# GLA recurrence and tanh-shrink MLP: fewer DMA pieces for w_in, another load order for unit 0, fewer warming products, new instruction orders

## The chip, the cores and the metric

The kernel runs on one core of one Trainium2 chip. The metric is the device time of one execution in microseconds; the median of three runs is given. Five engines matter: TensorE (PE in the profile; its weight loads are shown as PEld), VectorE (DVE), ScalarE (ACT), GpSimd (POOL) and SyncE (SP), which issues nearly all DMA transfers.

## The reference

```python
B, H, S, D = 4, 8, 768, 48            # d_model = H*D = 384, d_ff = 2048
for t in range(S):                    # gated linear attention
    state = alpha[:, :, t, :, None] * state + einsum('bhd,bhe->bhde', k[:, :, t], v[:, :, t])
    y[:, :, t] = einsum('bhd,bhde->bhe', q[:, :, t], state)
x = y.transpose(0, 2, 1, 3).reshape(B * S, H * D)
h = x @ w_in                          # (3072 x 384) @ (384 x 2048)
g = h - tanh(h)
out = g @ w_out                       # (3072 x 2048) @ (2048 x 384)
```

The inputs q, k, v and alpha are float32. w_in and w_out arrive as float64, seen as 64-bit integers, and are rebuilt as float32 on the chip.

## The kernel before

**Units and steps.** The 3072 tokens are cut into twelve units of 256 tokens (two chunks of 128), numbered 0 to 11. Each unit first passes the recurrence: turn or transpose alpha, k and q so that features lie on partitions (`turn aT`, `turn kT`, `turn qT` by TensorE for units 0 and 1, line 717; `flip` on DVE for the others, line 689); two scans along time on DVE (`U`, line 760, and `W`, line 779); k times U and q times W (line 729 or 784); then matmuls for scores, the update of the state and y. Then it passes eight MLP steps, numbered `u:s` (0:0 is unit 0, step 0). A step's first product is `first` (line 1242: twelve PE records, 2.59 us; plain form), ACT and DVE work on h (`square`, `cube`, `quad`, `shrunk`), and the second product follows (`second`, line 1322 for units 0 and 1, line 1344 afterwards with fewer multiplications). In all there are 96 steps.

**Weights.** w_in and w_out come in eight pieces each, `in0` to `in7` and `out0` to `out7`; a piece is 768 KB. `fetch` issues its DMA (line 42), ACT reads the raw words in two passes (`read`, lines 85 and 86), and DVE finishes the conversion in two more (lines 88 and 89). `first 0:s` needs `in<s>`, `second 0:s` needs `out<s>`. There are four raw buffers, so a fetch waits until DVE's first pass over the piece four places earlier is done. A piece of w_in is cut by tile and row range: eight DMAs of 96 KB. A piece of w_out is one DMA.

**Order.** The order of the work is written out by hand, or rather by a search whose result is stored: `Planner.STEPS` is a list of differences that gives the order in which all tasks are emitted, and so each engine's own order. The planner knows a cost (`us`) and a latency (`lat`) for each task. From them it works out starts only to decide where to put extra work on PE: `filler` is `spin`, a 128x128 product of the identity with itself (line 1428) whose result nobody reads. It fills PE's planned gaps until `y 0.0`. The before kernel has 36 spins: 8, then 2, 7, 10, 5, 2 and 2 at seven places.

**Loads of unit 0 and 1.** For unit 0 the loads of alpha, q, v and k, in this order, are issued in halves from SP and from ACT's queue. Then SP issues `in0`, and for unit 1 alpha, v, k, q, then `in1`, `in2`, `in3`. For units from 2 on (and alpha of unit 1) each of `ar`, `kr` and `qr` is loaded by four DMAs of 96 KB (line 607).

**DMA slots.** DMAs issued from SP and ACT share eight completion semaphores in turn. An issue waits until the transfer eight places before it has landed.

Of the kernel before, what the change touches and what calls it, by code (L numbers as in the profile page):

```python
# [17 lines left out]
HP = 64  # L18
# [19 lines left out]
def load_weight(nc, pool, rows, **kw):  # L38

    raw = pool.tile([P, WN], I64 if rows[0][2].dtype != FP32 else FP32, name="raw", **kw)  # L40
    for at, js, src in rows:
        nc.sync.dma_start(out=raw[at].rearrange("p (j n) -> p j n", n=src.shape[-1])[:, js], in_=src)
    return raw


def weight_parts(w_in, w_out, pad_rows, what, s, by_tile=True):

    if what == "out":
        return [(slice(0, P), slice(0, 2), w_out.rearrange("(j p) n -> p j n", p=P)[:, 2 * s:2 * s + 2, :])]
    parts = []  # L50
    for i in range(len(pad_rows[0])):
        at, f0 = pad_rows[0][i]
        step = pad_rows[1][i][1] - f0
        src = w_in[f0:f0 + len(pad_rows) * step].rearrange("(j p) n -> p j n", p=step)
        src = src[0:at.stop - at.start, :, 2 * s * P:2 * (s + 1) * P]

        few = at.stop - at.start < 32 or not by_tile
        parts += [(0, at, slice(0, len(pad_rows)), src)] if few else [(j - 9, at, slice(j, j + 1), src[:, j:j + 1]) for j in range(len(pad_rows))]
    return [x[1:] for x in sorted(parts, key=lambda x: (x[0], x[1].start))]
# [261 lines left out]
class Planner:  # L321
# [6 lines left out]
        "90 2 1 1 -3 9 -3 -1 -96 106 8 -11 -8 12 2 1 -6 4 -10 7 12 15 -14 -17 10 -12 20 -17 33 -23 8 -119 122 5 5 -20 8 8 5 -132 122 -9 27 -139 119 3 -9 27 -13 "  # L328
        "383 -382 13 -7 -11 -120 141 -2 3 -2 -10 -9 387 -510 134 16 -15 -130 506 -375 9 -8 9 -145 512 -366 365 -509 513 -2 -506 -4 144 369 -506 -5 512 5 -372 "
        "-2 3 367 -361 -149 -2 149 -142 506 -367 371 -514 511 8 -512 509 -1 -513 147 368 -367 -3 358 -500 -2 7 510 -514 520 -382 380 -511 508 1 -377 -137 504 "  # L330
        "11 4 -518 2 140 -135 512 4 -3 -517 140 -133 -5 139 377 -12 15 -518 2 5 512 5 -4 -517 519 -512 511 -516 505 -497 512 -519 2 132 386 4 -519 -2 7 511 "
        "-515 504 -502 125 389 3 -516 508 10 2 -3 -388 390 -392 387 -512 128 -4 397 -520 156 -24 394 -5 2 -398 397 -392 3 391 -365 374 -399 4 -10 16 383 -9 "
        "-387 403 -395 -10 400 -371 367 -365 359 9 3 -374 -21 400 3 -9 5 -400 2 395 8 -3 -376 381 -378 -24 404 -3 -351 356 -380 -4 -21 402 9 -380 -7 382 2 -382 "
        "25 -23 379 -406 411 -390 392 -17 -344 -49 405 -359 366 -387 375 -402 411 -408 410 -407 2 47 -30 383 -404 3 46 -48 4 -151 172 1 -3 388 -384 -173 174 "
        "-173 557 2 -1 -3 -554 189 -15 -25 1 -149 150 410 -2 -384 -2 387 -380 382 -369 371 -557 559 -3 -385 17 27 347 -4 -389 47 -42 -2 3 -5 14 376 3 2 -1 -350 "
        "-213 188 380 -349 -218 559 5 -373 2 382 -10 3 -348 -32 381 -3 -377 381 6 -4 -373 -4 383 -386 24 366 -5 -387 6 375 8 -385 379 -376 386 -3 -579 -8 581 "
        "-359 369 1 -410 42 -43 -172 585 3 -4 -410 46 375 -6 2 -5 -360 364 -371 360 -335 352 2 2 -404 50 341 5 -591 220 372 -370 374 6 -601 196 401 -377 26 346 "
        "7 3 -377 -2 377 4 -1 -353 -35 393 -3 -362 -242 221 384 11 -8 -412 -195 -12 621 2 -3 -3 -405 416 -6 -621 629 -6 10 -376 371 2 1 -619 629 -7 -621 625 -3 "
        "-11 18 -6 7 1 -7 11 -23 -416 436 4 -10 12 -1 3 -7 -14 -425 3 -196 198 -4 5 26 401 12 -637 639 -419 421 -420 427 -6 2 -1 -642 644 -423 424 3 -647 649 "
        "-1 -18 21 -453 23 -24 40 -14 18 413 -455 451 -426 15 399 17 2 -428 40 -25 417 -660 267 388 -406 -2 422 -8 -4 -656 662 -419 418 3 -14 25 -6 -12 -385 "  # L340
        "-31 430 -28 33 -6 -402 2 -26 436 -29 -650 662 -416 436 -6 1 -676 663 -416 423 -427 428 -15 -384 410 2 -461 460 -6 2 -15 -438 -5 1 2 -223 247 417 23 "
        "-439 -247 683 1 10 -7 2 -1 3 -443 447 2 -1 5 -700 264 4 -44 24 -247 248 420 -403 435 4 -408 -47 458 -437 25 393 -12 -400 -5 430 1 -430 436 6 -713 695 "
        "-472 485 -484 485 -27 -410 417 25 -438 -23 443 22 -450 422 -390 -299 701 -406 2 -24 423 13 6 -12 -453 464 -4 6 -444 449 -473 -247 250 -2 4 465 10 -6 "
        "-468 -252 278 21 422 1 -448 453 -25 29 -3 -453 454 -20 14 1 -723 716 13 2 -730 274 442 16 -440 -40 -1 43 -41 24 446 -424 434 -732 738 -5 1 -412 -48 30 "
        "-27 458 -453 454 10 -745 738 -770 772 -1 3 34 -24 -6 -5 7 -452 29 404 18 -424 430 -10 14 -3 -18 -442 461 -754 748 11 -438 434 -6 8 9 -466 460 -432 433 "
        "-462 -2 465 -464 478 -9 -24 34 -8 2 -3 -467 477 -452 468 -44 13 32 -827 811 -476 461 16 16 -26 -12 23 16 -25 10 16 -15 16 1 -16 17 -16 28 -11 -15 -22 "
        "49 -28 17 -15 17 -1 3 8 -26 42 -58 43 -10 26 -24 9 16 -59 44 16 -15 16 -15 16 1 -16 17 -16 28 -11 -15 -34 61 -28 -32 49 -15 27 -10 -564 563 12 -9 -18 "
        "28 -62 -513 -3 517 -516 578 -574 528 34 13 -574 563 12 -549 -4 554 -48 -505 563 19 -28 -48 58 -57 48 28 -27 9 -43 44 -9 27 -17 -44 62 -27 10 18 -62 63 "
        "-18 19 -18 19 -18 -46 65 -18 -571 573 -1 18 -16 1 16 8 -582 -16 -24 563 -562 622 -59 -538 589 -16 -597 622 -59 -538 598 -59 -522 -14 586 -584 594 -9 "
        "-36 -509 555 -45 -540 586 1 13 -59 -512 -43 556 46 -30 -553 554 30 12 -10 28 -17 -42 33 -32 29 13 -27 -567 611 -16 -27 -542 557 13 16 -43 -574 575 43 "  # L350
        "-16 -573 590 -16 1 -14 30 -593 -20 -24 638 -634 618 17 -637 621 28 -632 589 32 -15 -599 626 -28 17 -621 649 -26 10 -44 61 -16 -44 -583 644 -16 -44 31 "
        "30 -16 -30 19 28 -16 -45 46 16 -624 625 1 -17 -634 602 61 -28 -16 45 -61 33 1 28 -61 17 45 -61 47 15 -61 32 30 -15 28 -683 671 -12 13 -16 28 -43 -17 "
        "33 28 -12 -48 61 -688 660 -32 48 -669 655 16 -1 12 -60 -605 -16 1 681 -706 660 -634 -25 30 676 -661 -44 706 -47 48 -47 1 -621 668 10 18 -24 -35 -605 "
        "637 -31 41 18 -44 -14 31 10 -678 696 -58 41 -651 669 -17 18 -17 18 -30 13 32 -14 -671 654 -31 49 -30 -635 617 31 -30 48 -17 30 -712 652 48 -47 60 -29 "
        "46 -16 -12 -33 14 32 -45 61 -30 -695 710 16 -47 -14 1 61 -729 713 -688 705 -16 -32 33 16 -732 700 -672 705 -735 719 17 -33 1 44 -62 51 -17 29 -62 -686 "
        "737 28 -44 28 -62 79 -78 62 -9 -21 47 -16 -47 34 14 -47 63 -46 17 -736 750 -748 749 -31 46 -63 34 30 -63 48 16 -63 64 -16 2 -778 777 16 -49 35 -781 5 "
        "801 -803 793 -49 -741 801 17 -823 797 -1 11 -8 -772 4 732 -16 77 -76 33 27 -780 797 -61 34 28 -17 -44 35 10 17 -61 62 -17 1 17 -16 17 -16 -785 802 -15 "
        "-1 17 4 -3 9 -795 720 -735 -25 -1 24 752 61 -26 -809 852 -26 10 -811 750 35 43 -16 -61 -746 824 -809 793 -61 78 -16 17 -63 64 -17 -13 -786 817 -17 18 "
        "-17 -48 78 -29 -815 817 15 -31 32 -17 29 -10 -68 -766 -3 770 66 12 -63 54 -19 29 16 -860 816 29 -64 80 -79 -781 11 834 16 -79 64 16 -15 16 -31 16 16 "
        "-850 851 1 -68 51 -829 779 -781 782 78 -28 17 -66 51 -18 -18 63 -11 28 -901 20 865 -8 -55 34 18 -847 859 -11 -17 -35 79 -15 -866 803 -796 812 48 15 "  # L360
        "-62 63 -45 30 -863 864 -14 -852 881 -63 64 -63 48 16 -63 48 -863 865 -16 30 -902 887 -33 -853 888 -887 853 48 -47 34 -33 47 10 -890 882 26 -27 10 -42 "
        "35 -883 891 -9 -33 -848 891 -42 34 24 -57 -849 907 -918 902 -886 859 44 -16 17 -44 97 -52 -17 1 17 -16 17 -16 28 -11 -15 -32 1 58 -28 17 28 -43 27 -10 "
        "-33 32 12 16 -59 16 18 10 -43 32 27 -15 -43 59 -26 11 16 -15 16 1 -16 17 -16 30 -13 -15 -34 63 -30 -32 49 -15 -33 50 12 16 -29 3 -51 33 -17 62 -28 12 "
        "-45 35 11 16 -61 46 -45 61 1 -16 17 -16 17 -16 17 -16 -969 986 -15 -1 17 -15 17 8 -9 3 -56 -932 -4 937 -935 997 -1000 939 36 26 -61 62 15 -25 11 -47 "
# [64 lines left out]
def fast(tc, q, k, v, alpha, moe_w_in, moe_w_out, out, w_in, w_out, ident, ok, pad_rows):  # L429
    nc = tc.nc  # L430
# [1111 lines left out]
```

## Time and profile before

| | |
|---|---|
| Three runs | 564.53, 565.50, 565.52 us; median 565.5 us |
| The profiled execution | 566.18 us; its span from first to last instruction is 564.5 us |
| Busy in the span | PE 553.1 us (98%), PEld 502.9, DVE 463.9, ACT 358.7, POOL 4.9 |
| Mean granted TensorE clock | 0.993 |
| DMA | 50.90 MB in 60717 packets, mean 90 GB/s |
| Products of `spin` | 36 |

Busy time is the time in which an engine has an instruction in it; for PE the ends of matmuls are modelled. "Idle before, releaser" in a row tells how long the engine had nothing to do and which instruction's end let it go on. A matmul of float32 stands as two records, so 8 spins are a row of x16. A busy PE is not the same as useful PE: spins count as busy.

### The profile page before, as it was taken

How to read it: one execution, taken by the hardware profiler on the slowest of the kernel's cores; microseconds unless marked ns; L12 is line 12 of the kernel's file. 1: busy time of each engine (PE TensorE's matmuls, PEld its weight loads, DVE VectorE, ACT ScalarE, POOL GpSimd, SP SyncE). 2: the span in 40 equal slices, each digit the busy share in tenths (PEclk: the TensorE clock that was granted, in tenths of full speed). 3: DMA queues.
4: the chain of work that ended last, by engine and by line, in shares of the span. 5: the costliest groups of instructions: out<-in, count | busy, mean ns of one | idle time of the engine just before them, and what ended most of it. 6: DMA issues, size and time to landing. Idle time of an engine off the chain costs nothing.

```text
span 564.5 us, 14803 instructions
## 1 busy us (share of the span) xinstructions
PE 553.1 (98%) x6029; PEld 502.9 (89%) x6029; DVE 463.9 (82%) x855; ACT 358.7 (64%) x723; POOL 4.9 (1%) x23
## 2 busy tenths in 40 slices
PE   8989999999999999999999999999999999999995
PEld 8877777678999999999999999899999999999994
DVE  6879789999997598796996779999979975765764
ACT  2579988737876668777575446857745555455550
POOL 3000000000000000000000000000000000000000
PEclk9989999999999999999999999999999999999998
DMA  7777873229464275563430013031110000000001
GB/s 197 209 211 220 273 189 113 59 64 198 92 143 126 88 134 137 141 160 97 130 107 1 31 35 88 29 83 38 32 36 2 29 9 1 30 9 1 28 1 35
DMA packets 60717, 50.90 MB, mean 90 GB/s; under 512 B 35776, under 2 KB 50400, under 8 KB 60640
## 3 DMA queue, kind: packets, MB, share of 16 engines
q1 hardware_dynamic: 57728, 48.88, 33.2%
q10 hardware_dynamic: 2912, 0.98, 0.7%
q8 instruction: 49, 0.80, 0.6%
q14 instruction: 28, 0.23, 0.1%
HBM read 44.04 MB, written 4.72 MB: 86 GB/s over the span
## 4 chain that ended last, share of the span: by engine, by line
PE 94%; DVE 3%; issue 1%; ACT 0%; POOL 0%; DVEq 0%; ACTq 0%; POOLq 0%
PE o L1344 32%; PE h L1242 22%; PE h L1253 13%; PE o L1322 7%; PE h L1274 7%; PE h L975 4%; PE spin L1428 2%; PE sc L948 2%; PE sc L1121 1%; PE sc L955 1%; PE sc L975 1%; PE turned L717 1%; DVE same L1407 1%; DVE W L779 0%; DVE U L760 0%
## 5 line engine op out<-in xcount | busy, mean ns | idle before, releaser
L1242 PE MATMUL h<-xT,w_in 128*128 128x256 f32 (+1 forms) x588 | 132.9, 380 | 1.7 <-DVE w_in L89 1.6
L1242 PEld LDWEIGHTS h<-xT,w_in 128*128 128x128 f32 x588 | 109.8, 192 | 18.0 <-DVE w_in L89 2.7
L1344 PE MATMUL o<-b,e 128*128 128x192 f32 x480 | 94.2, 326 | 0.0
L1344 PEld LDWEIGHTS o<-b,e 128*128 128x128 f32 x480 | 78.8, 191 | 0.2
L1344 PE MATMUL o<-w_out,e 128*128 128x192 f32 x320 | 78.8, 328 | 0.0
L1298 DVE SCALAR_TENSOR_TENSOR g<-z,w 128x512 f32<-128x512 f32 x96 | 65.2, 681 | 4.3 <-ACT z L1289 1.6
L1344 PE MATMUL o<-b,g 128*128 128x192 f32 x320 | 68.4, 326 | 0.0
L1279 DVE TENSOR_TENSOR w<-h,u 128x512 f32<-128x512 f32 x48 | 32.9, 686 | 36.7 <-PE h L1274 36.7
L1289 ACT ACTIVATE z<-u 128x512 f32<-128x512 f32 x96 | 60.1, 629 | 1.8
L1285 ACT ACTIVATE u<-w 128x512 f32<-128x512 f32 x48 | 30.2, 630 | 41.3 <-DVE w L1279 41.3
L1253 PE MATMUL h<-xT,w_in 128*128 128x128 f32 x288 | 55.5, 279 | 0.9 <-DVE w L1279 0.6
L1344 PEld LDWEIGHTS o<-w_out,e 128*128 128x128 f32 x320 | 55.1, 190 | 1.3
L1253 PE MATMUL h<-xT,w_out 128*128 128x128 f32 x288 | 54.1, 275 | 0.0
L1344 PEld LDWEIGHTS o<-b,g 128*128 128x128 f32 x320 | 54.0, 190 | 0.1
L1285 ACT ACTIVATE u<-h 128x512 f32<-128x512 f32 x48 | 28.3, 592 | 40.0 <-PE h L1242 39.7
L1253 PEld LDWEIGHTS h<-xT,w_in 128*128 128x128 f32 x288 | 48.4, 190 | 4.2 <-DVE w L1279 1.5
L1266 ACT COPY u<-h 128x128 f32<-128x128 f32 x96 | 24.5, 265 | 43.0 <-PE h L1253 42.6
L1304 ACT ACTIVATE big<-u 128x1024 f32<-128x1024 f32 x48 | 50.6, 1054 | 0.5
L1274 PE MATMUL h<-xT,w_in 128*128 128x256 f32 x192 | 49.0, 380 | 0.0
L1311 DVE TENSOR_TENSOR e<-g 128x384 f32<-128x384 f32 x80 | 44.0, 550 | 3.4 <-PE o L1344 1.1
L1294 DVE TENSOR_TENSOR w<-h,u 128x512 f32<-128x512 f32 x48 | 32.7, 680 | 15.0 <-ACT u L1285 15.0
L1253 PEld LDWEIGHTS h<-xT,w_out 128*128 128x128 f32 x288 | 44.3, 192 | 0.1
(167 smaller groups left out, 979.9 us busy)
## 6 DMA issues: line engine op xcount, KB each, us to landing
raw<-in_moe_w_out_dram SPq DMA_DIRECT2D x16, 768.0 KB, 5.3
raw<-in_moe_w_in_dram SPq DMA_DIRECT2D x80, 96.0 KB, 3.7
raw<-in_moe_w_in_dram SPq DMA_DIRECT2D x16, 288.0 KB, 5.2
vt<-in_v_dram SPq DMA_DIRECT2D x23, 192.0 KB, 3.6
ar<-in_alpha_dram SPq DMA_DIRECT2D x44, 96.0 KB, 2.3
qr<-in_q_dram SPq DMA_DIRECT2D x40, 96.0 KB, 2.3
kr<-in_k_dram SPq DMA_DIRECT2D x40, 96.0 KB, 2.2
out_dram<-cross SPq DMA_DIRECT2D x19, 96.0 KB, 1.7
```

The lines of the kernel that those rows point to most:

```text
L1242: T.matmul(h[:, a, to], lhsT=w_in[:, j, f * P:(f + 1) * P], rhs=xT[u][:, j, to], start=(j == 0), stop=(j == KT - 1))
L1253: T.matmul(m["h", s][:, to], lhsT=left[n][:, s], rhs=right[u][n], start=start, stop=True, skip_group_check=True)
L1274: T.matmul(m["h", s][:, 2 * a:2 * a + 2].rearrange("p i t -> p (i t)"), lhsT=wi[:, KT - 1, s, a], rhs=xT[u][:, KT - 1, :], start=False, st ...
L1279: V.tensor_add(m["w", s], m["h", s].rearrange("p i t -> p (i t)"), m["u", s])
L1285: A.activation(m["u", s], m["h", s], AF.Square, scale=W_SCALE ** -1.5)
L1289: A.activation(m["z", s], m["u", s], AF.Square, bias=QB, scale=QA * W_SCALE)
L1294: V.tensor_mul(m["w", s], m["h", s], m["u", s])
L1298: V.scalar_tensor_tensor(out=g.rearrange("p a c t -> p (a c t)"), in0=m["z", s], scalar=QK, in1=m["w", s], op0=ALU.add, op1=ALU.mult)
L1304: A.activation(big, m["us", s // 2].rearrange("p s t -> p (s t)"), AF.Relu, bias=-U_FAST, scale=W_SCALE, accum_out=over[:, n:n + 1])
L1311: V.tensor_sub(e[:, 0:3, :], x[:, 3:4].to_broadcast([P, 3, P]), x[:, 0:3])
L1322: T.matmul(m["o"][c], lhsT=g[:, a, c, :], rhs=w_out[:, f, :], start=(f == 0), stop=(f == FT - 1))
L1344: T.matmul(o[n][:, i], lhsT=g_, rhs=w_, start=(s_ == 0 and (n, i) in ((0, 0), (1, 0), (2, 1), (3, 0))), stop=(s_ == FS - 1), skip_group_ch ...
```

## The change

- `load_weight` and `weight_parts`: a piece of w_in is six DMAs rather than eight. For the two ranges of 48 rows, tile 0 is one DMA of 96 KB and tiles 1 and 2 together one of 192 KB; the two ranges of 16 rows stay as they were. Of piece `in0` alone, the two DMAs of the upper range of 48 rows (partition 64) are issued from ACT's queue.
- `load`: `ar`, `kr` and `qr` take two DMAs of 192 KB per load rather than four of 96 KB.
- `filler`: another rule for the number of spins. The program now has 23: 7 ahead of `turn aT 0`, 15 ahead of `back 0.0`, 1 ahead of `update 0.0`.
- New planner costs for loads and fetches, `turn aT 0` at 1.5, and one more planned dependency for `scores 1.0`.
- `STEPS` is new. Among much else: unit 0 is loaded as alpha, k, q, v; unit 1 as q, alpha, k, v; the three turns of unit 0 stand one after another; ACT reads `in0` before it copies `kn` of chunk 0.0 (line 1039), DVE finishes `in0` before it masks the scores of 0.0, `in1` before `kU` of unit 1 and `in2` before the `W` scan of unit 1; PE runs `first 0:1` before `back 1`, and `first 0:3` and `second 0:0` before `scores 1.0`.

Besides these, each engine has the same instructions as before: PE's only other count is the 13 spins, DVE's is the same, ACT has two more DMA issues, SP 96 fewer.

```diff
-def load_weight(nc, pool, rows, **kw):
+def load_weight(nc, pool, rows, both=False, **kw):
     for at, js, src in rows:
-        nc.sync.dma_start(out=raw[at].rearrange("p (j n) -> p j n", n=src.shape[-1])[:, js], in_=src)
+        (nc.scalar if both and at.start % HP == 0 and at.start else nc.sync).dma_start(
+            out=raw[at].rearrange("p (j n) -> p j n", n=src.shape[-1])[:, js], in_=src)
...
-        parts += [(0, at, slice(0, len(pad_rows)), src)] if few else [(j - 9, at, slice(j, j + 1), src[:, j:j + 1]) for j in range(len(pad_rows))]
+        parts += [(0, at, slice(0, len(pad_rows)), src)] if few else [(j - 9, at, slice(j, k), src[:, j:k]) for j, k in ((0, 1), (1, len(pad_rows)))]
...
     STEPS = (
-        "90 2 1 1 -3 9 -3 -1 -96 106 8 -11 -8 12 2 1 -6 4 -10 7 12 15 -14 -17 10 -12 20 -17 33 -23 8 -119 122 5 5 -20 8 8 5 -132 122 -9 27 -139 119 3 -9 27 -13 "
+        "90 1 1 2 -1 2 -95 100 -3 9 -10 7 11 -7 27 -30 6 -1 -4 27 -34 -97 98 18 16 -32 11 -4 10 17 -33 17 -117 135 -17 -117 139 -14 -15 8 -10 12 6 14 -28 9 "
...
-                filled += [(free, -1, do, None)] * int(gap / (1.5 * us) if free == self.begin.get(engine) else (gap + 0.3) / us if gap > 0.2 else 0)
+                filled += [(free, -1, do, None)] * int(gap / (1.75 * us) if free == self.begin.get(engine) else gap / us - 1 if gap > 2 * us else 0)
...
+    BOTH_QUEUES = 1
...
-            raw_of[what, s] = load_weight(nc, raw_pool, weight_parts(moe_w_in, moe_w_out, pad_rows, what, s), bufs=4)
+            raw_of[what, s] = load_weight(nc, raw_pool, weight_parts(moe_w_in, moe_w_out, pad_rows, what, s), both=what == "in" and s < BOTH_QUEUES, bufs=4)
...
-                for g in (0, NP // 2):
-                    nc.sync.dma_start(out=t[HP * r:HP * r + 32, g:g + 2].rearrange("p g t d -> p g (t d)"),
-                                      in_=src[head(g, r):head(g, r) + 2].rearrange("g (i n) -> i g n", i=32))
+                nc.sync.dma_start(out=t[HP * r:HP * r + 32].rearrange("p g t d -> p g (t d)"),
+                                  in_=src[head(0, r):head(0, r) + NP].rearrange("g (i n) -> i g n", i=32))
```

## The prediction

> **What bounds the kernel now.** I read the page's busy row and slices first, then the sums by stretch, then the order in time of PE, DVE and SP over the first 60 us, and the waits.
>
> ```profile
> PE 553.1 (98%) x6029; PEld 502.9 (89%) x6029; DVE 463.9 (82%) x855; ACT 358.7 (64%) x723; POOL 4.9 (1%) x23
> ...
> PEclk9989999999999999999999999999999999999998
> ```
>
> PE is busy for 98% of the span, and the clock row shows one dip, in the third slice.
>
> ```profile
> 31.05:37.66 6.61, 4.65 (x18) 3.54 (x17) 4.64 (x8) 4.91 (x9) 0.00 (x0) 0.74 0.86 242
> 37.66:45.00 7.34, 7.26 (x210) 6.01 (x209) 5.65 (x11) 6.27 (x10) 0.00 (x0) 1.00 0.57 172
> 45.00:557.70 512.70, 511.82 (x5245) 467.12 (x5245) 428.92 (x791) 334.01 (x683) 0.00 (x0) 1.00 0.31 81
> ```
>
> These are sums by stretch: length, then busy time of PE, PEld, DVE, ACT, POOL, then granted clock, DMA share, GB/s. From 45 us to the last product at 557.7 PE lacks only 0.88 us. The change leaves PE's instructions there as they are, so what is won must come mainly from the first 45 us, by handing PE the same work earlier. From 31.05 to 37.66 PE idles 2 us and its clock is 0.74.
>
> ```profile
> 1.57 3.79 PE L1428 MATMUL spin<-ident 128*128 128x128 f32 x16 [1.57 <-POOL ident masks.py:199]
> 5.28 1.89 PE L717 MATMUL turned<-ident,rough 64*64 64x64 f32 x64
> ...
> 8.84 1.83 PE L1428 MATMUL spin<-ident 128*128 128x128 f32 x14
> 10.59 1.55 PE L717 MATMUL turned<-ident,rough 64*64 64x64 f32 x64
> 12.07 2.50 PE L1428 MATMUL spin<-ident 128*128 128x128 f32 x20
> 14.41 0.55 PE L1034 MATMUL y<-ident,kT 112*128 112x112 f32 x4
> ...
> 29.60 1.60 PE L1242 MATMUL h<-xT,w_in 128*128 128x128 f32 x12
> 31.05 0.55 PE L1121 MATMUL y<-ident,kT 112*128 112x112 f32 x4
> 31.97 0.60 PE L1121 MATMUL y<-ident,kT 112*128 112x112 f32 x4 [0.37 <-DVE kT L729]
> 34.15 4.54 PE L1242 MATMUL h<-xT,w_in 128*128 128x256 f32 x12 [1.58 <-DVE w_in L89]
> ```
>
> PE in order of time: start, length, operation. Four losses stand here. Ten spins hold `back 0.0` until 14.41, though its input is ready at 12.76:
>
> ```profile
> 12.09 0.67 DVE L729 TENSOR_TENSOR kT<-turned,U 128x512 f32<-128x512 f32 x1
> ...
> 33.14 0.96 DVE L89 CUSTOM_DVE_ANT_0 w_in<-bits,more 128x1536 uint16<-128x1536 uint16 x1 [0.17 <-DVE bits L88]
> ```
>
> The second turn (k, loaded last, landed at 9.37 by the DMA records) lasts 1.55 against 1.16 for that of q. `first 0:1` waits 1.58 us for `in1`, which DVE finishes only at 34.1 though its bytes landed at 25.03. And that product takes 4.54 us where the form takes 2.59: after the idle stretch the clock stood at 0.50 for 3.41 us (34.24 to 37.66).
>
> **Part by part: start.** A cold spin costs (3.71 - 0.26)/8 = 0.43 us; a warm one 0.245 (ten from 12.07 to 14.41, seven from 8.84 to 10.59, five in 1.23). Spins before: 3.71 + 0.64 + 1.75 + 2.34 + 1.23 + 0.64 + 0.82 = 11.13 us from start to next start. After: 7 cold 3.28, 15 warm 3.68, one 0.25, sum 7.21. Removed: 3.92 us. Whether PE then works or idles is decided by DVE's chain, so I follow it.
>
> `turn aT 0` starts at 5.28 - 0.43 = 4.85 (alpha landed at 4.31, no wait) and ends its 1.83 at 6.68. DVE's copy, its two scans, ends and first W follow as before, 0.43 earlier, plus one moved memset (0.07): `kUa` at 12.09 - 0.43 + 0.07 = 11.73, `qWa` 12.31, `kUb` 12.97, W 13.55, `qWb` 14.7 to 15.4. k is now the second load and lands when q did, 5.55, so turn kT runs 6.68 to 7.83 and turn qT to 8.95; 15 spins end at 12.63. `back 0.0` at 12.63, `scores 0.0` 13.07 to 14.17, spin, `update 0.0` to 15.02, turn qT 1 waits for `qWb` (0.5 idle) to 16.6, `back 0.1` 17.05, `scores 0.1` 18.15. DVE converts `in0` first (1.45), then masks 16.8 to 18.0: in time. `y 0.0` 19.75, update 20.35, carried 21.7, `y 0.1` 23.3, turn kT 1 24.4, two halves of `first 0:0` (1.54 each) 27.5. Then `first 0:1`: before at 34.15, now at 27.5 if `in1` is done. DVE: `aT 1` and second mask to 21.5, state, U 24.1, `in1` 25.6: done. So 6.65 us earlier, less `back 1` (0.95), which now follows it: 5.7. The cold 1.95 goes: 7.65. New: `first 0:3` waits some 0.45 for `in3` (DVE: `kU` and `ends` 27.1, `in2` 28.6, cube, W 31.9, cube, `in3` 34.1; PE is there at 33.7). Gain by 45 us: **7.2**. The same by losses: 3.92 + 0.39 + 0.37 + 1.58 + 1.95 - 1.0 of new waits = 7.2.
>
> [...] The row: PE idled 0.37 and 1.58 us inside one stretch of 3.4 us, and the clock fell for 3.41 us. [...] by the row, gaps adding to 2 us already cost 1.95. I take the row: 23 spins suffice only while the gaps around 12 to 17 us stay below that, as worked out (0.6). If not, 7.2 becomes about 4 (1.95 and the gap itself).
>
> **Loads.** `in0` must have landed by 11.2, because ACT now reads it (1.97) ahead of `kn` 0.0, behind which `update 0.0` and all of ACT queue. Before it landed at 13.23:
>
> ```profile
> 4.32 6.64 SPq L42 DMA_DIRECT2D raw<-in_moe_w_in_dram  x8
> 11.01 1.84 SPq L607 DMA_DIRECT2D ar<-in_alpha_dram  x4
> ```
>
> ```profile
> 9.00:12.00 3.00, 2.93 (x78) 2.67 (x78) 2.93 (x8) 1.16 (x2) 0.00 (x0) 1.00 0.56 142
> ```
>
> Eight issues took 6.64 us, because the last waited for the slots of v and k (8.0 and 9.4), and the engines were only 0.56 busy at 9 to 12 us against 1.14 (290 GB/s) at 7 to 9. Now its six wait for slots of alpha, k and q (to about 6.9), two of them on ACT before that has other work (its copy of aT comes at 6.8). The bytes are the same 2.36 MB; 1.92 were moved by 9 us, and the rest at 290 GB/s ends at 10.6. I take 11.2. [...] The 0.56 says issue time is what lacked, so I keep 7.2.
>
> `in1` then has 2.36 MB more to come, before 11.8 us for it with SP issuing every 0.46 us 96 KB; at 0.9 of the rate that the engines reached it lands at 20 to 21, and ACT reads it from 20.3. One us late still fits, since ACT idles before `x 0.1` at 23.4. `ar` of unit 1 follows q on SP at about 10.4 and, with the 2.5 to 3.7 us that its parts took, is there by 15, just before ACT widens it at 15.4. For the later units I cost the halved issues nothing: SP waits 161 us for `cross` alone, so issue time isn't short there; without that cover a late load would hold DVE's flip by its lateness. POOL's queue is not touched. Piece pairs: before, nine DMAs went round eight slots, so a piece's last part waited for the `out` before it (one set of eight issues took 5.56 us for 3.7 of issuing); now seven, which no longer meet. PE wants a pair each 5.17 us. The pairs landed some 6.8 us apart from `out0` (38.3) to `out4` (65.3), with `second 0:0` 9.5 us behind `out0`. Now SP reaches `out0` at about 23.5; with the 7.4 us that it took before it lands at 31 and is wanted at 36.8: cover 6 us. At 6.8 us a pair against the 5.5 that PE really used (`second 0:0` at 47.7, `second 0:4` at 69.9) four pairs eat 5.2 of it. So I cost it nothing, but barely.
>
> **After 45 us.** At most 3.1 us can be had: 0.88 idle and eleven refills where twelve products last 2.78 rather than 2.59. The other end, the new order loses as much, +3.1. The new order is again free of forced idle as far as the chain above goes; I take -1.5, half the upper end. The tail (557.7 to 564.5, 6.8 us) has the same instructions: 0.
>
> **Sum.** -7.2 - 1.5 = -8.7 against a span of 564.5 (the profiled execution took 566.18, 1.7 more; the median is 565.5, so that execution is 0.7 slow). Span 555.8; median 565.5 - 8.7 = **556.8**.
>
> **Rivals.**
> Clock falls again: the trace's own example; for it, 13 fewer spins; against, gaps of 0.6. Gain 4 + 1.5 = 5.5 or so: 560.0. Chance 0.15.
> Loads decide (`in0` late by 1.9, or pairs above 7 us apart, where the cover of 6 us is eaten over four pairs; at 8 us it costs 4): gain 3 to 5.3: 561.0. Chance 0.11. Here also belongs that the spins turn into plain idle time: then only 4.3 - 1.0 is won, 562.2.
> More: the late refills go too and DVE's conversions pack as planned: 553.5. Chance 0.10.
> Slower: DVE becomes late at each step. It has 428.9 busy of 512.7 after 45 us, and 15.0 of 15.0 at 105 to 120; PE then waits for DVE to free the bank of h. With 96 steps, it decides from 8.7/96 = 0.09 us a step; at 0.1 the kernel is at 566.4. Against: the same DVE instructions, and before only 0.01 a step was visible. Chance 0.04.
> No difference: 0.02. The forecast keeps 0.58, with 554.8 to 558.8.
>
> **Numbers.** A measurement of this kernel can tell 0.2%, 1.1 us, from no change. Range 552.5 to 561.5: below lies almost nothing, above it half the loads' case and the slower one. Faster 0.94, same 0.02, slower 0.04.
>
> **What would show it.** Right: `turn aT` at 4.9, `back 0.0` at 12.6, `first 0:1` near 27.5 lasting 2.6, no clock below 1.00 between 7 and 550 us, `in0` landed by 11.5. Wrong: a row of idle before `update 0.0` from ACT `kn`; a wait of DVE `w_in` or `w_out` ahead of products at 35 to 75 us; PE idle above 1 us after 45.

## The result and the profile after

The change brings 2.8 us: 562.51 us median (560.73 to 563.50, seven runs) against 565.34 (563.96 to 565.52, seven runs); the ratio is 0.9952, 95% interval 0.9934 to 0.9970. Forecast were 556.8 us and a range of 552.5 to 561.5. The direction is right, the size is a third of the forecast, and the median lies above the range. A second series of the same kernel (experiment 1) gave 561.75.

The profiled execution of after took 560.73 us, span 558.9. It is the fastest of its runs (1.78 below the median), and that of before was 0.84 above its own, so the two traces lie 5.45 us apart where the medians lie 2.83 apart. One difference between them matters for all that follows: the trace of before has an early fall of the clock (0.50 from 34.24 to 37.66 us), that of after has none (1.00 from 4.86 us to 550) (see "The clock of every execution" below).

The page of after: busy time, and the granted clock in 40 slices.

```profile
PE 545.1 (98%) x6003; PEld 496.8 (89%) x6003; DVE 469.3 (84%) x855; ACT 358.4 (64%) x723; POOL 4.9 (1%) x23
...
PEclk9999999999999999999999999999999999999998
...
q8 instruction: 49, 0.80, 0.6%
```

The 26 records of the 13 spins are gone, and so is the clock's dip in the third slice. SP issues 294 DMAs against 374 in before, 80 fewer rather than the 96 given with the change. The last line, a DMA queue with packets, MB and share, plays no part in the prediction; it will matter below.

The sums by stretch of after: length, busy time of PE, PEld, DVE, ACT and POOL, granted clock, DMA share, GB/s.

```profile
9.00:12.00 3.00, 1.31 (x13) 1.23 (x12) 2.93 (x10) 1.21 (x3) 0.00 (x0) 1.00 1.03 204
12.00:15.00 3.00, 3.00 (x34) 2.74 (x33) 2.96 (x6) 1.56 (x2) 0.00 (x0) 1.00 1.16 257
...
25.00:45.00 20.00, 16.75 (x163) 13.37 (x156) 15.63 (x25) 17.74 (x27) 0.00 (x0) 1.00 1.01 261
45.00:552.00 507.00, 507.00 (x5352) 464.43 (x5350) 432.33 (x790) 329.89 (x679) 0.00 (x0) 1.00 0.31 78
```

Two things to see: after 45 us PE now lacks nothing, and from 25 to 45 us it idles 3.25 us, where 0.45 was forecast. The DMA share is above 1 from 9 to 15 us (1.03 and 1.16), at 204 and 257 GB/s; the forecast let the engines carry 290.

PE of after in order of time:

```profile
1.57 3.35 PE L1429 MATMUL spin<-ident 128*128 128x128 f32 x14 [1.57 <-POOL ident masks.py:199]
4.86 2.10 PE L718 MATMUL turned<-ident,rough 64*64 64x64 f32 x128
6.77 1.33 PE L718 MATMUL sc<-ident,rough 64*64 64x64 f32 x64
8.04 2.16 PE L1429 MATMUL spin<-ident 128*128 128x128 f32 x17
11.89 1.61 PE L1429 MATMUL spin<-ident 128*128 128x128 f32 x13 [1.69 <-issue]
13.34 0.55 PE L1035 MATMUL y<-ident,kT 112*128 112x112 f32 x4
...
15.86 0.67 PE L1048 MATMUL y<-vt,kn 128*64 128x48 f32 x16 [0.47 <-ACT kn L1040]
...
25.21 0.49 PE L1243 MATMUL h<-xT,w_in 128*128 128x128 f32 x2
27.20 3.16 PE L1243 MATMUL h<-xT,w_in 128*128 128x128 f32 x24 [1.49 <-DVE w_in L90]
31.06 2.42 PE L1243 MATMUL h<-xT,w_in 128*128 128x256 f32 x10 [0.71 <-DVE w_in L90]
...
37.91 2.86 PE L1243 MATMUL h<-xT,w_in 128*128 128x256 f32 x12 [1.05 <-DVE w_in L90]
40.60 2.74 PE L1323 MATMUL o<-w_out,g 128*128 128x384 f32 x8
```

Behind the start PE stops five times, 5.41 us together; the forecast had two stops of 1.0 together, 0.5 ahead of `turn qT 1` and 0.45 ahead of `first 0:3` (the last of the five). The first stands in the middle of a run of spins, which wait for nothing that the profile shows ("issue"). The third is odd: `first 0:0` stops after two records. `back 0.0` comes at 13.34 (forecast 12.6), `second 0:0` at 40.60 (36.8).

The waits of after up to 45 us (engine, line, whom it waits for: total, times, longest), and ACT's two long ones in order of time:

```profile
ACT more L86 <- DMA raw<-in_moe_w_in_dram: 7.2, 4, 3.0
...
PE h L1243 <- DVE w_in L90: 3.2, 3, 1.5
...
DVE w_in L90 <- PE h L1243: 2.2, 2, 1.3
```

```profile
13.44 1.08 ACT L86 ACTIVATE more<-raw 128x768 int16<-128x768 uint32 x1 [2.96 <-DMA raw<-in_moe_w_in_dram]
...
24.15 1.09 ACT L86 ACTIVATE more<-raw 128x768 int16<-128x768 uint32 x1 [2.81 <-DMA raw<-in_moe_w_in_dram]
```

`in0` is there at 13.4 (forecast 11.2, before 13.23), `in1` at 24.1 (20 to 21; before 25.03). ACT stands before both. And PE and DVE wait for each other over w_in: the second and third line of the waits.

### The profile page after: what moved, and what is told of

Same layout as the page of the kernel before. It is cut to its first block, busy times and chain, and to the rows that moved or that the text cites. A ratio compares the mean times of both kernels' runs of the same rounds, so it can differ in the third digit from the quotient of the medians.

```text
span 558.9 us, 14579 instructions
## 1 busy us (share of the span) xinstructions
PE 545.1 (98%) x6003; PEld 496.8 (89%) x6003; DVE 469.3 (84%) x855; ACT 358.4 (64%) x723; POOL 4.9 (1%) x23
## 4 chain that ended last, share of the span: by engine, by line
PE 94%; DVE 1%; SPq 1%; issue 1%; DMA 1%; ACT 0%; POOL 0%; ACTq 0%; DVEq 0%; POOLq 0%
PE o L1345 32%; PE h L1243 23%; PE h L1254 14%; PE o L1323 7%; PE h L1275 7%; PE h L976 4%; PE sc L949 2%; PE sc L1122 1%; PE sc L956 1%; PE sc L976 1%; SPq L42 1%; DMA raw<-in_moe_w_in_dram 1%; PE spin L1429 1%; SPq L593 1%; DVE w_in L90 1%
## 5 line engine op out<-in xcount | busy, mean ns | idle before, releaser
L1243 PEld LDWEIGHTS h<-xT,w_in 128*128 128x128 f32 x588 | 108.1, 190 | 19.9 <-DVE w_in L90 4.2
L1280 DVE TENSOR_TENSOR w<-h,u 128x512 f32<-128x512 f32 x48 | 33.1, 690 | 25.3 <-PE h L1275 24.6
L1254 PEld LDWEIGHTS h<-xT,w_in 128*128 128x128 f32 x288 | 47.9, 190 | 1.8
L1323 PE MATMUL o<-w_out,g 128*128 128x384 f32 x128 | 43.4, 489 | 0.0
```

The source lines that it names most:

```text
L1243: T.matmul(h[:, a, to], lhsT=w_in[:, j, f * P:(f + 1) * P], rhs=xT[u][:, j, to], start=(j == 0), stop=(j == KT - 1))
L1254: T.matmul(m["h", s][:, to], lhsT=left[n][:, s], rhs=right[u][n], start=start, stop=True, skip_group_check=True)
L1280: V.tensor_add(m["w", s], m["h", s].rearrange("p i t -> p (i t)"), m["u", s])
L1323: T.matmul(m["o"][c], lhsT=g[:, a, c, :], rhs=w_out[:, f, :], start=(f == 0), stop=(f == FT - 1))
```

## The experiments

The theory after the result: three things took the expected gain, namely the landing of the pieces of w_in (DMA time; theory L), PE's stop among the spins, and the mutual wait of PE and DVE (theory I, the interlock). The rival: only the spins bring anything, and the new order and the transfers are worth nothing or cost. Medians are given with the ratio to before in the same series (before was 564.7 to 564.9 in all four); the edits are against after unless stated.

**1. after_same: after unchanged.**

> The changed kernel once more, unchanged, for a second trace of it. Both theories: 562.5 us (560.7 to 563.5). The two traces are to show what differs between executions: when the TensorE clock is released (4.9 us in the first trace), and when in0 to in3 have landed (13.4, 24.1, 27.5 and 31.4). If loads decide (theory L), the waits of PE for w_in (3.2 us in the first trace) are there again within 0.5 us.

Measured: 561.75 us (559.90 to 563.75), 0.9941 [0.9919, 0.9964]. This time the profiled execution is the slowest, span 561.9. Its PE in order of time, and a stretch of it:

```profile
8.56 2.16 PE L1429 MATMUL spin<-ident 128*128 128x128 f32 x17
12.68 2.34 PE L1429 MATMUL spin<-ident 128*128 128x128 f32 x13 [1.96 <-issue]
14.82 0.95 PE L1035 MATMUL y<-ident,kT 112*128 112x112 f32 x4
```

```profile
12.00:18.00 6.00, 5.32 (x46) 4.80 (x47) 5.52 (x9) 2.52 (x3) 0.00 (x0) 0.72 1.01 231
```

The same stop after the same 17 records of the run, longer by 0.27, and behind it the clock is 0.50 from 13.36 for 3.41 us: the same products take 2.34 rather than 1.61. So "the clock falls again" does happen to this kernel in some executions, behind a gap that the prediction did not know. PE's waits for w_in are there again, 3.0 us.

**2. after_contig: w_in laid out piece by piece.** DVE of after, its last pass over `in1` and over `in2`:

```profile
26.18 0.96 DVE L90 CUSTOM_DVE_ANT_0 w_in<-bits,more 128x1536 uint16<-128x1536 uint16 x1 [1.42 <-ACT more L87]
...
30.04 0.96 DVE L90 CUSTOM_DVE_ANT_0 w_in<-bits,more 128x1536 uint16<-128x1536 uint16 x1 [0.92 <-PE h L1243]
```

`first 0:0` reads `in0` alone, and `in0` was finished at 16.4; yet it goes on at 27.20, when the pass over `in1` has ended (27.14). And the pass over `in2` waits for PE's products, which read other pieces. In the tile `[P, KT, d_ff]` a piece takes 256 columns out of each of the three row tiles, so that the address range from its first to its last element covers parts of the other pieces. That this is what ties them together is the theory; the new layout tests it.

```diff
-    w_in = consts.tile([P, KT, d_ff], FP32, name="w_in")
+    w_in = consts.tile([P, FT // 2, KT, 2 * P], FP32, name="w_in")
...
-lhsT=w_in[:, j, f * P:(f + 1) * P]
+lhsT=w_in[:, s, j, a * P:(a + 1) * P]
```

> w_in is laid out piece by piece in SBUF, so that no piece's bytes lie between those of another; nothing else is changed. Theory I (interlock: products of an earlier step wait for a later piece, and DVE's last pass over a piece waits for products that read another piece): first 0:0 no longer waits for in1 (1.5 us on PE), DVE's waits for PE ahead of w_in (2.2 us) are gone, and the kernel is 1.3 to 2.5 us faster than the changed one, about 560.5. Theory L (the landing of in1 to in3 alone decides): the waits move to first 0:1 and first 0:3 and the time is within 0.5 us of 562.5.

Measured: 559.83 us (559.50 to 560.43), 0.9913 [0.9897, 0.9930]. PE of this kernel:

```profile
25.12 1.60 PE L1243 MATMUL h<-xT,w_in 128*128 128x128 f32 x12
26.94 4.20 PE L1243 MATMUL h<-xT,w_in 128*128 128x128 f32 x24 [0.21 <-ACT xT L1030]
...
37.16 2.83 PE L1243 MATMUL h<-xT,w_in 128*128 128x256 f32 x12 [1.52 <-DVE w_in L90]
```

`first 0:0` runs through; two of PE's three waits for w_in are gone, the last has grown, and DVE no longer waits for PE ahead of w_in (2.2 us in after). So the interlock is real and costs after about 1.9 us (561.75 less 559.83, same series; the intervals of the two ratios still overlap a little).

**3. before_contig: the same layout in before** (the diff of 2).

> The same layout of w_in in the kernel before. DVE waited 3.2 us for PE ahead of w_in there. Theory I: these waits go; PE stood for it only at first 0:2, so 0.3 to 1.0 us faster than before, about 564.8. Theory L: no change, 565.3.

Measured: 564.93 us, 0.9992 [0.9977, 1.0006]: nothing. DVE's waits of 3.2 us for PE are gone there too, but with the old order they cost PE no time: its one wait for w_in is 1.56 against 1.58 in before. Only the new order loses by the interlock.

**4. after_half: half of the bytes of in0 to in3.** The two 192 KB transfers of each of these pieces (tiles 1 and 2 of the two ranges of 48 rows, half of the piece's bytes) are left out, and GpSimd writes zeroes in their place.

```diff
+        if less and js.start == 1:
+            nc.gpsimd.memset(... [:, js], 0)
+            continue
```

> Leaves out the 192 KB transfers of tiles 1 and 2 (both ranges of 48 rows) of in0 to in3; GpSimd zeroes these words instead, so 1.5 of 3.1 MB are not moved early on and the product uses zeros there. Theory L: in0 lands at about 12, in1 at 21, in2 at 23, in3 at 26; ACT's waits for in-pieces (7.2 us) nearly vanish, PE's waits for w_in (3.2 us) too, and the kernel is 3 to 4 us faster than the changed one, about 559. Theory I: landings come earlier but PE's waits for w_in stay above 2 us, and it gains 1 us or less.

Measured: 558.89 us (558.26 to 559.36), 0.9894 [0.9876, 0.9912]. The pieces land at about 10.9, 20.7, 22.9 and 25.5 us instead of 13.4, 24.1, 27.5 and 31.4. So bytes, or the DMA time that they take, set the landings, and are worth 2.9 us. The layout here is that of after, and its PE still waits 2.2 us for w_in.

**5. before_six: the load part of the change alone**, on before.

```diff
-for j, k in ((0, 1), (1, 2), (2, 3))
+for j, k in ((0, 1), (1, len(pad_rows)))
...
+    BOTH_QUEUES = 1
...
-                for g in (0, NP // 2):
-                    nc.sync.dma_start(out=t[..., g:g + 2] ...)
+                nc.sync.dma_start(out=t[...] ...)
```

> The load part alone: the kernel before with w_in in six transfers a piece, two of in0 on ACT's queue, and ar, kr, qr in two; orders and spins stay. Theory L (the DMA engines' time per packet sets the landings, not the number of issues): in0 lands within 1 us of before (13.2), in1 to in3 within 1 us of 25.0, 28.7 and 33.1, no change in time, 565.0. Theory N (issues and slots set them, as the prediction had it): in0 lands at about 11 and in1 to in3 some 3 us earlier; but with the old orders only the wait at first 0:1 could use it, so up to 1 us faster.

Measured: 565.77 us, 1.0016 [1.0004, 1.0028]. The stretch from 9 to 12 us of this kernel, columns as above:

```profile
9.00:12.00 3.00, 2.89 (x79) 2.64 (x76) 2.93 (x8) 1.36 (x3) 0.00 (x0) 1.00 1.07 212
```

The DMA share rises from 0.56 (before, same stretch) to 1.07: the issue is earlier, as meant. But `in0` lands at 15.1, later than in before (13.23). Here the fuller engines did not bring the piece earlier.

**6. after_eight: the load part taken back in after** (the diff of 5 reversed); spins and orders are those of after.

> The load part undone in the changed kernel: eight transfers a piece, all on SP, and four each for ar, kr, qr; orders, loads' order and spins stay. Theory L: the landings move by less than 1 us, the time by less than 1 us (562.5). Theory N: in0 to in3 land 2 to 3 us later than in the changed kernel, PE's waits for w_in grow by as much, 564.5 to 565.5.

Measured: 562.85 us, 0.9968 [0.9956, 0.9980]; PE waits 4.3 us for w_in in its trace, one of them 2.31, against 3.2 in after. ACT reads `in0` from 13.38 (13.44 in after), `in1` from 24.93 (24.15) and `in3` from 33.01 (31.43): the load part did not move `in0`, the piece that it was made for, and the later ones by 0.8 to 1.6 us. After's own ratios are 0.9952 and 0.9941, 0.9 to 1.5 us better, but the intervals overlap; a worth of the load part is not shown.

**7. before_newspins: the spin rule alone**, on before: 22 spins (7, 5, 7, 3) instead of 36.

```diff
-int(gap / (1.5 * us) if free == ... else (gap + 0.3) / us if gap > 0.2 else 0)
+int(gap / (1.75 * us) if free == ... else gap / us - 1 if gap > 2 * us else 0)
```

> The spin part alone: the kernel before with the new rule for spins (22 rather than 36: 7, 5, 7 and 3); orders and loads stay. The prediction's step (ten spins hold back 0.0 by 1.6 us, and the later ones by more): y 0.0 starts 1.5 to 2.5 us earlier; but first 0:1 waits for in1, which DVE takes up after the scans, so 1 to 2 us faster, about 563.5. The rival (spins only turn into idle time): no change, or a fall of the clock with 1.7 us lost, 565 to 567.

Measured: 561.61 us (560.74 to 564.41), 0.9944 [0.9925, 0.9962]. One line of the rule brings as much as the whole change. PE of this kernel:

```profile
10.54 1.83 PE L1428 MATMUL spin<-ident 128*128 128x128 f32 x14
12.47 0.60 PE L1034 MATMUL y<-ident,kT 112*128 112x112 f32 x4
...
17.50 0.85 PE L906 MATMUL y<-pm,v_gap 128*32 128x128 f32 x12
...
31.54 4.33 PE L1242 MATMUL h<-xT,w_in 128*128 128x256 f32 x12 [1.59 <-DVE w_in L89]
```

`y 0.0` starts at 17.50 instead of 20.79, and `first 0:1` still waits and meets a clock of 0.50 from 31.14, as in before.

**8. order_alone: the new orders alone**, with the loads and the spin rule of before: 30 spins (8, 17, 3, 2). The counts of 44 and 31 in the text on record are wrong; before has 36 and after 23.

```diff
-for j, k in ((0, 1), (1, len(pad_rows)))
+for j, k in ((0, 1), (1, 2), (2, 3))
...
-int(gap / (1.75 * us) if free == ... else gap / us - 1 if gap > 2 * us else 0)
+int(gap / (1.5 * us) if free == ... else (gap + 0.3) / us if gap > 0.2 else 0)
```

> The new orders of unit 0's steps alone: the pieces of w_in come in eight transfers and the loads of rows and of w_out's first chunks as before, and the spin rule is the one of before, which gives 30 spin products at these orders (8, 17, 3, 2) against 44 in before and 31 in after. Theory A (the new orders net to about nothing: what they save is spent in waits for w_in and in the stop of instruction issue, and the gain of the whole change is that of the spin products): 562.5 to 563.5 us, 0.995 to 0.998 of before, because the new orders bring fewer spins with them whatever the rule. Rival (the new orders cost time by themselves, the new spin rule wins it back): 564.5 us or more.

Measured: 562.34 us (561.12 to 564.80), 0.9961 [0.9948, 0.9975], just under the 562.5 to 563.5 of theory A. With 6 and 7 this gives a square, all with eight transfers a piece:

| | 36 or 30 spins, old rule | 22 or 23 spins, new rule |
|---|---|---|
| old orders | 1 | 0.9944 [0.9925, 0.9962] |
| new orders | 0.9961 [0.9948, 0.9975] | 0.9968 [0.9956, 0.9980] |

By the ratios each alone gives 2.2 to 3.2 us, and both together give 1.8. The sum in the prediction added them.

**9. after_spread: where PE's stop comes from.** The second run of spins broken up: 7, 4 and 4 ahead of the turns of a, k and q, 7 ahead of `back 0.0`, 1 later; 23 as in after (the "31" on record is a slip).

```diff
-filled += [...] * int(gap / (1.75 * us) ...)
+filled += [...] * {'turn aT 0': 7, 'turn kT 0': 4, 'turn qT 0': 4, 'back 0.0': 7, 'update 0.0': 1}.get(name, 0)
```

> After with its 31 spin products spread otherwise: 7 ahead of turn aT as now, 4 ahead of turn kT, 4 ahead of turn qT, 7 ahead of back 0.0 and 1 ahead of update 0.0, 23 in all; loads and orders as in after. Theory A (the stop of 1.2 to 2.0 us inside the second run of spins is a stop of instruction delivery in the short, equal products of a spin run, and the fall of the clock follows it when the stop is long): with the run broken by turns the stop is under 1 us, the clock does not fall, and the median is 560.5 to 561 us. Rival (the stop comes at a fixed count of instructions or a fixed time, whatever stands there): the stop is still 1.2 us or more, and the median stays at 562 to 562.5 us.

Measured: 562.09 us, 0.9948 [0.9930, 0.9966]. The theory of the text fell, its rival held. PE of this kernel:

```profile
10.89 0.38 PE L1429 MATMUL spin<-ident 128*128 128x128 f32 x1
13.23 2.94 PE L1429 MATMUL spin<-ident 128*128 128x128 f32 x13 [1.96 <-issue]
```

The stop is unchanged, and now follows the first record of a run. What is equal is the count: here 14+64+8+64+8+64+1 = 223 PE records come before it, in after 14+128+64+17 = 223. In all twelve of the eighteen traces in which PE starts record 223 before 11 us, it stops behind it (and in before_six, where it starts it at 11.68). In each of them the first packet on the queue `q8 instruction` of the page lands shortly before PE goes on. 49 such packets of 16 KB make up its 0.80 MB; in after 122 records of PE start between one landing and the next (the mean from the fourth on; single ones up to 220):

| kernel | packet lands, us | record 224 starts, us | gap before it, start to start |
|---|---|---|---|
| before | 10.60 | 11.82 | 0.29 |
| before_newspins | 10.04 | 11.43 | 0.11 |
| after | 10.47 | 11.89 | 1.97 |
| after_same | 11.40 | 12.68 | 2.24 |
| after_spread | 11.87 | 13.23 | 2.33 |
| both_spread | 10.80 | 12.15 | 1.50 |

In the thirteen with a stop, record 224 starts 1.2 to 1.6 us behind the landing. That PE is waiting for its own instructions there is the author's reading of these two times; no trace names what it waits for. Before has no stop: PE starts record 223 only at 11.52, 0.92 us behind the landing.

**10. after_idle: do loads hold that packet up?** v of unit 0 and `in0` are fetched behind q of unit 1, and what needs them moves behind.

```diff
+        for what, past in [('fetch in0', 'load qT 1'), ('load v 0', 'load qT 1'), ('gaps 0.0', 'natural 0.0'),
+                           ('read in0', 'gaps 0.0'), ('in0', 'masked 0.0')]:
+            order.remove(names[what])
+            order.insert(order.index(names[past]) + 1, names[what])
```

> After with unit 0's v and piece in0 fetched only behind unit 1's q, so that hardly any load is under way from 7 to 10 us, with the steps that need them moved behind (gaps 0.0, read in0, in0); the same 23 spins. Theory L (the packet of TensorE's instructions waits behind loads): it starts before 8.5 us, and the stop at the 223rd record is under 0.3 us. Rival (the packet is asked for late, whatever the loads do): it starts at 9 us or later and the stop is 1.2 us or more. Either way v and in0 come some 4 us later, and the kernel should be 1 to 4 us slower than after: 563.5 to 566.5 us.

Measured: 561.93 us (560.83 to 563.11), 0.9951 [0.9924, 0.9978]. PE of this kernel:

```profile
8.11 2.16 PE L1432 MATMUL spin<-ident 128*128 128x128 f32 x17
10.80 1.61 PE L1432 MATMUL spin<-ident 128*128 128x128 f32 x13 [0.52 <-issue]
```

The packet starts at 8.31 and lands at 9.44, and record 224 at 10.80 is the earliest of all eighteen traces. Theory L gave under 8.5 (met) and a stop under 0.3 (0.52 to be seen); the rival's 9 us and 1.2 us are both missed. So with v and `in0` fetched later the packet landed 1.0 and 2.0 us earlier than in the two traces of after (10.47 and 11.40), in one trace of this kernel; what sets the rest of its time stays open. The kernel was not slower (563.5 to 566.5 had been expected), though v and `in0` came later; why is open.

**11. contig_v1late: layout by pieces, and v of unit 1 loaded behind in3** (192 KB twice, out of the way of `in1` to `in3`). To the diff of 2 comes, with the same three lines as in 10:

```diff
+        for what, past in [('load v 1', 'fetch in3')]:
```

> The changed kernel with w_in piece by piece in SBUF, and v of unit 1 loaded after in3 rather than before in1, so that 0.39 MB less stand ahead of in1. Theory L: in1 to in3 land 1.5 us earlier, PE's waits ahead of first 0:1 to 0:3 shrink by 1 to 1.5, time 558.5 against 559.8 with the layout alone. Theory N or the interlock alone: within 0.4 us of 559.8.

Measured: 560.52 us (558.09 to 562.32), 0.9927 [0.9899, 0.9955]. `in1` lands at about 22, `in3` at 28.7, and the waits for w_in are nearly gone from its trace (span 556.4), but the median does not improve on the layout alone; its runs spread over 4 us. Three of the six show a lower clock (see below).

**12. contig_both: besides, in0 is read after `kn`** on ScalarE and finished after the mask on VectorE; 24 spins.

```diff
-        for what, past in [('load v 1', 'fetch in3')]:
+        for what, past in [('load v 1', 'fetch in3'), ('read in0', 'natural 0.0'), ('in0', 'masked 0.0')]:
```

> After with w_in's rows laid out piece by piece, the load of unit 1's v moved behind the fetch of in3, and the read of in0 moved up by two steps on ScalarE and its second half on VectorE ahead of the scores' mask. 24 spin products. Theory A (three waits cost after its gain: interlocked pieces, full DMA engines, the order of ScalarE's read): PE's waits for w_in up to 45 us come to under 1 us and the median is 558 to 559 us. Rival (the stop of instruction issue and the clock decide what is left): 559.8 to 560.5 us as with the layout alone.

Measured: 561.06 us (558.80 to 562.22), 0.9939 [0.9916, 0.9961]: above theory and rival. Its profiled execution, the fastest of its runs (span 557.1), has no wait of PE for w_in before 40 us:

```profile
12.68 1.61 PE L1432 MATMUL spin<-ident 128*128 128x128 f32 x13 [1.62 <-issue]
14.12 0.55 PE L1038 MATMUL y<-ident,kT 112*128 112x112 f32 x4
```

Its slower runs have no trace; six of the eight show a lower clock (see below).

**13. both_spread: the same with 18 spins** (7, 4, 4, 3, spread over the turns).

```diff
+filled += [...] * {'turn aT 0': 7, 'turn kT 0': 4, 'turn qT 0': 4, 'back 0.0': 3}.get(name, 0)
```

> The kernel before this one in the list with its spin products spread: 7 ahead of turn aT, 4 ahead of turn kT, 4 ahead of turn qT, 3 ahead of back 0.0, 18 in all. Theory A (stop inside a run of spins): no stop over 1 us, no fall of the clock, 557 to 558 us. Rival (the stop stays wherever PE's first hundred products end): within 0.5 us of the kernel that it is made from.

Measured: 558.74 us (558.08 to 559.84), 0.9902 [0.9875, 0.9928], the best complete kernel of the study. PE:

```profile
10.65 0.38 PE L1432 MATMUL spin<-ident 128*128 128x128 f32 x1
12.15 0.71 PE L1432 MATMUL spin<-ident 128*128 128x128 f32 x5 [1.12 <-issue]
12.70 0.55 PE L1038 MATMUL y<-ident,kT 112*128 112x112 f32 x4
...
18.62 0.85 PE L910 MATMUL y<-pm,v_gap 128*32 128x128 f32 x11 [0.42 <-issue]
...
24.66 5.54 PE L1246 MATMUL h<-xT,w_in 128*128 128x128 f32 x36
...
36.77 2.74 PE L1326 MATMUL o<-w_out,g 128*128 128x384 f32 x8
```

The stop is still there (1.12), so the expectation's reason is wrong, and that its size was nearly right is luck. `back 0.0` starts 1.4 us earlier than in contig_both (12.70 against 14.12): some 0.9 because 5 spin records instead of 13 stand behind the stop, 0.5 because PE went on earlier in this execution (12.15 against 12.68; the packet landed at 10.80 against 11.35). `second 0:0` starts at 36.77, the time that the prediction gave for after, but by other means. And a second stop (0.42, in the middle of `y 0.0`) comes 126 records behind the first and ends 1.27 us after the second packet has landed (17.35), as the first stop ends 1.35 us behind the first packet.

**14. both_cut: 15 spins (7 and 8), all ahead of record 223.**

```diff
+filled += [...] * {'turn aT 0': 7, 'back 0.0': 8}.get(name, 0)
```

> The kernel with w_in by pieces, v of unit 1 behind in3 and in0 read later, with 15 spins: 7 ahead of turn aT and 8 ahead of back 0.0, so that TensorE's first 222 records are spins and turns and the 223rd is useful. Theory (spins behind the instruction packet cost their length, those before it are free): back 0.0 starts at 11.8 to 12.4 us instead of 14.12, and the median is 558 to 558.7 us, as with the 18 spread spins (558.74). Rival (fewer spins let the clock fall): a fall of 3.41 us in the trace and 559.5 us or more.

Measured: 560.10 us (558.83 to 561.86), 0.9922 [0.9895, 0.9950]. PE of this kernel:

```profile
12.59 0.60 PE L1038 MATMUL y<-ident,kT 112*128 112x112 f32 x4 [1.49 <-DVE kT L733]
```

`back 0.0` starts at 12.59, later than expected, because DVE finishes its input only at 12.53; so this run does not test whether spins ahead of the packet are free. Its trace has a fall of the clock at 14.46 for 3.41 us: the rival's case. Fewer spins than in both_spread buy no time at the start (12.59 against 12.70).

**15. after_v0late: v of unit 0 loaded behind in0**; 23 spins as in after.

```diff
+        for what, past in [('load v 0', 'fetch in0')]:
```

> After with unit 0's v loaded behind in0 rather than ahead of it; the same 23 spins. Theory (the landing of in0 is set by the bytes ahead of it, 384 KB of v among them): in0 is there by 11.5 to 12.2 us instead of 13.1 to 13.8, ScalarE waits for it 1.5 us less, and as in1 still lands at 24, the median is 561.5 to 562.5 us. Rival (it is set by the issue slots or by its own descriptors): in0 lands at 13 us as before.

Measured: 561.39 us (560.09 to 562.91), 0.9937 [0.9921, 0.9954]. Inconclusive on its question: the last transfer of `in0` landed at 12.93, near the rival's 13, but half of v was issued ahead of it after all (ACT's queue, 5.21), and ACT then waited 6.6 us for v before it could read `in0` at 14.80.

**16. best: both_cut with the move of 15 too.**

> The same with unit 0's v behind in0 as well. If in0 lands earlier by some 1.5 us and in1 with it by nothing, 557.5 to 558.5 us; if v comes too late for update 0.0 (TensorE idle ahead of it by over 0.5 us), 559 us.

Measured: 560.52 us (559.66 to 561.32), 0.9926 [0.9901, 0.9951]. `update 0.0` waits 1.05 us: the bad case of the expectation, and 1.5 us worse than it said.

**The clock of every execution.** Each execution's mean granted clock is on record. An early fall of 3.41 us at 0.50 takes 0.003 off it (half of 3.41 us in a span of some 560): the eight traces with one have 0.991 to 0.996, the ten without 0.996 to 0.999. So a mean of 0.995 or less is taken as the mark of a fall (0.996 can be either). Executions, and their median in us, for ten of the kernels:

| kernel | 0.995 or less | 0.996 or more |
|---|---|---|
| before, all four series | 34: 565.8 | 87: 564.2 |
| after, both series | 9: 562.5 | 5: 561.8 |
| before_newspins | 3: 563.2 | 9: 561.4 |
| order_alone | 2: 563.5 | 19: 562.2 |
| after_eight | 16: 563.3 | 5: 561.7 |
| after_contig | 0 | 6: 559.8 |
| contig_v1late | 3: 562.1 | 3: 559.1 |
| contig_both | 6: 561.3 | 2: 560.0 |
| both_spread | 1: 559.8 | 5: 558.6 |
| both_cut | 3: 559.5 | 3: 560.1 |

Executions with the mark have the higher median by 0.8 to 3 us (not in both_cut; by 0.3 to 1.5 in the kernels left out). Most executions of before do not have it, and most of after do. In the right column alone the interlock is still worth 1.9 us, the two edits of the square give 2.9 and 2.0 alone and 2.6 together, and the load part (after against after_eight) gives nothing.

## Why the prediction was wrong, step by step

Two terms of the sum failed. The new waits, put at 1.0 us, are 5.41: by 45 us the profiled pair gains 3.7 of the forecast 7.2, because PE comes 0.8 late to `first 0:0` and then waits 2.8 us more for w_in than foreseen. And the 1.95 us of the cold product were taken from one execution: it is a loss of a minority of the executions of before (34 of 121 bear the mark of a fall), and after has falls of its own (9 of 14 bear it). Without the mark, before has 564.2 and after 561.8.

- **Spins removed, 3.92 us: right in size, wrong to add.** Alone they move `y 0.0` by 3.29 and the median by 3.1 (experiment 7). With the new orders the smaller count adds nothing (square in 8).
- **Losses of before (0.39, 0.37, 1.58, 1.95): gone in the trace of after, as said; what was late next was mis-sized.** The waits of 5.41 are 1.69 behind record 223, 0.47 before `update 0.0`, 1.49, 0.71 and 1.05 for w_in. Of the lateness of `second 0:0` against the forecast (3.8 us), about 0.8 is there at `first 0:0` (25.21 against 24.4), and 2.8 are the three waits for w_in (3.25) less the 0.45 that was foreseen for them.
- **`back 0.0` at 12.63: missed by 0.7, by a stop not in the sum.** The turns ran faster than forecast, the spins began at 8.04 rather than 8.95, and all of it was lost at record 223. The trace of before could not show it as a loss: it has 0.29 us there, in the turn whose length of 1.55 the prediction put beside the landing of k at 9.37, 1.2 us before that turn began.
- **`in0` by 11.2: the step of the chain that failed first.** It landed at 13.4. The forecast rested on one number, the DMA share of 0.56 from 9 to 12 us, read as a lack of issues. The share did rise, to 1.03, and the landing did not move (13.23 in before). The 290 GB/s taken for the rest were those of 7 to 9 us in before; after reaches 204 and 257 at a share above 1, and from 10.0 us on unit 1's q and alpha, issued behind `in0`, shared the engines.
- **`in1` at 20 to 21: 24.1.** `in2` and `in3` follow at 27.5 and 31.4. Halving the bytes brings `in1` to 20.7 (experiment 4), so it is again the DMA time of the bytes.
- **"`first 0:1` at 27.5, `in1` done": missed the interlock.** 1.9 us (experiments 2 and 3). A trace of it stood in the waits of before, DVE's last pass over w_in waiting 3.2 us for PE's h, and was not followed up.
- **Clock: the row was right.** A fall came with a gap of 1.96 us in experiment 1, as with gaps of 0.37 and 1.58 in before. But the case was given 0.15 because gaps of only 0.6 were foreseen. And the row itself was a fall that most executions of before do not have, so its 1.95 should not have been taken off a median.
- **After 45 us, -1.5: right.** Counting the same work done (each form of product at its mean cost), the profiled pair gains 3.7 us by 45 us and 1.9 behind. PE idles nothing after 45 us, and `second 0:0`, at 40.60, does not wait for `out0`, which ACT reads from 35.12: the cover held.
- **Rivals.** "Loads decide" gave 561.0, with the remark that spins turned into idle time give 562.2. At 562.5 measured, that remark came closest, in a case given 0.11, and "Clock falls again" (0.15) is, by the mark, true of most executions of after besides; the forecast's 0.58 was too much for a chain of some ten forecast starts, each of which needs the one before it.

Shown by runs: the interlock, the worth of the spin rule and of the orders, that they do not add, that bytes (or their DMA time) set the landings, that PE's stop comes behind the same count of records, 223, and ends 1.2 to 1.6 us behind the packet's landing. Shown by the clocks on record, without an experiment of its own: that slower executions of a kernel mostly have a lower clock (the mark goes with 0.8 to 3 us in most of the table). Open: how much of the missing gain the stop costs by itself, since every kernel with after's orders has it or another wait in its place, and why the clock falls oftener in contig_both (6 of 8) than in both_spread (1 of 6).

## What to carry to other kernels

When idle padding and waits are removed at once, do not add their gains: work out the arrival of the next input, and stop the sum there; here two edits worth 3.2 and 2.2 us alone were worth 1.8 together. A low DMA share (0.56) beside a late landing (13.23) showed here only that issue was late; the share rose to 1.03, and the landing, 13.4, did not follow. Before a loss seen in one trace is taken off a median, ask how many executions have it. And follow up a pair of waits in which two engines name each other over one tile: look whether pieces of it lie inside each other's address range.

## What the runs showed of the hardware

- PE's stop: in the thirteen traces with one behind record 223, the next record started at 10.8 to 13.2 us, 1.2 to 1.6 us behind the landing of the first packet on `q8 instruction` (after: landing 10.47, record 224 at 11.89). The earliest, 9.44 and 10.80, came where v of unit 0 and `in0` were fetched later (experiment 10, one trace). No wait of a semaphore shows there; the profile names it "issue". What holds PE there was not shown beyond these times.
- The clock's early falls: before first has 1.00 at 6.94 us and falls to 0.50 at 34.24, for 3.41 us; its gaps of 0.37 and 1.58 end at 31.97 and 34.15. In after_same the fall at 13.36 comes behind a gap of 1.96 that ends at 12.68; in before_newspins one at 31.14 lies in a gap of 1.59 that ends at 31.54. After has 1.00 from 4.86 us to 550 and no early fall, though it has a gap of 1.69. The length of a gap does not decide alone: 1.84 us came without a fall in after_contig, and 1.49 with one in both_cut. What else decides is open.
